# Dense attention beside sliding-window attention on one core: PV in groups of four column tiles, and dense matmuls placed by a count of active rows

## The chip, the core and the metric

The kernel runs on one core of a Trainium2 chip. A core has five engines that run side by side, each in its own program order: TensorE (PE, matrix products), VectorE (DVE), ScalarE (ACT), GpSimd (POOL) and SyncE (SP, which here only issues DMAs). They wait for one another through semaphores. PE writes into PSUM, eight banks of 128 partitions by 512 fp32 numbers; the other operands lie in SBUF.

The metric is the device time of one execution in microseconds, lower is better.

## The reference

Two attentions over 2048 positions and 448 features, with 16 heads of 28 features each; their outputs stand side by side in one result of 2048 x 896.

```python
def _A_ref(x, wq, wk, wv, wo):          # one key head and one value head for all 16 query heads
    q = (x @ wq).reshape(B, S, H, Dh).transpose(0, 2, 1, 3)
    k = x @ wk
    v = x @ wv
    p = softmax(einsum("bhqd,bkd->bhqk", q, k) * Dh ** -0.5)
    o = einsum("bhqk,bkd->bhqd", p, v)
    return o.transpose(0, 2, 1, 3).reshape(B, S, H * Dh) @ wo

def _B_ref(x, wqkv, wo):                # each position sees itself and 7 earlier ones, 2 apart
    q, k, v = heads of (x @ wqkv)
    kg, vg = k and v gathered at pos - 2 * w, w = 0..7
    attn = softmax(where(mask, einsum("bhsd,bhswd->bhsw", q, kg) * Dh ** -0.5, -1e9))
    return heads joined of einsum("bhsw,bhswd->bhsd", attn, vg) @ wo
```

Part A has 16 x 2048 x 2048 scores, all of which go through an exponential. Part B has eight scores a position and head.

## The kernel before, in words

**A planner writes each engine's program.** `Gen` lists every instruction (or small group of them) as an `Op` with an engine, an assumed duration, what it reads and writes, a priority `pr` and an earliest time `rel`. `Sched.run` then plays the program on a model of the five engines: whichever engine is free first takes the ready op with the lowest `pr`. The order found there is the order in which the engine executes, whatever the real durations turn out to be. `Sched.resolve` adds the semaphore waits.

**PSUM.** Part A's scores go into banks 0 to 2 and 3 to 4 in turn (`SLOTS`), its PV sums into bank 5 (`PVBANK`). Everything else shares banks 6 and 7 (`XBANKS`): a `Use` is one tenancy of such a bank, from its first PE op to its last reader.

**Part A** (`a_loop`, L655). There are 1024 units (sc, t, tb, j): 4 chunks of 512 queries, 4 groups t of four heads, 16 blocks of 128 keys, 4 heads j in a group. A unit is one scores matmul of 32 rows (a head's features) by 512 columns, and one PV matmul of 128 rows, 512 columns and 32 result columns. The units are cut into groups of three and of two, after the two slots. For each group n:

- the scores (L677): two or three matmuls, each in its own quarter of PE's rows, written to the slot's banks;
- the exponential (L688) on ACT, over 1536 or 1024 columns, out of PSUM into one of eight buffers (`expT`, `ERING`);
- PV (L702): the group's matmuls, each in its own quarter of PE's columns, added into bank 5. Where a group straddles two quads (a quad is the 64 units of one sc and t), PV is cut in two ops.

At the end of a quad `a_quad_end` copies bank 5 out (L722), sums the denominators (L727, Use "D"), inverts and spreads them (L733, L735), and scales (L741, L746); after every fourth quad come the output products (L758). Queries for the next chunk are projected by `a_q` (L629, L643).

**Part B** runs beside it in 16 blocks of 128 positions: projections of queries and keys for four blocks at a time (`b_qk`, L799) and of values (`b_v`, L815), products of queries and shifted keys on DVE (L840), their sums over a head by PE (`b_logits`, L847, 32 tiny matmuls a block), softmax, weighted values on DVE (L891), their sums by PE (L900), the output product (L907). Block k gets its earliest times from `T = B0 + BSTEP * k`.

**The start.** Ten matmuls on a tile of zeros (L535), A's first 512 positions transposed by PE, keys (`a_head`, L559), the value projection (`a_v`, L598), the keys' bias term (Use "KG", L604).

**Fills.** PE's granted clock depends on its recent work, so ahead of a scores group the planner may put one matmul whose result nobody reads (L675): if the dense ops that it booked in the last 2.2 us sum to under 0.3 us.

Of the kernel before, what the change touches and what calls it, by code (L numbers as in the profile page):

```python
# [12 lines left out]
D = 448  # L13
H = 16
DH = 28
KC = 112
NCH = 4
NSB = 16
WIN = 8
# [5 lines left out]
NU = 4 * 4 * 16 * 4  # L25
SLOTS = ((0, 1, 2), (3, 4))
EW = 512 * max(len(x) for x in SLOTS)
ERING = 8
# [29 lines left out]
class Use:  # L58


    def __init__(self, name, banks, late=False):
        self.name = name
        self.banks = banks
        self.late = late
        self.bank = None
        self.ops = []
        self.left = 0
        self.pe_left = 0


class Sched:
    LAT = 0.13
    OWN = 0.06
# [30 lines left out]
    def run(self, engines):  # L104
# [13 lines left out]
        recent = []  # L118

# [24 lines left out]
        while left:  # L144
# [3 lines left out]
            for (r, o) in cand[e]:  # L148
                bank = None
                if o.use is not None and o.use.bank is None:  # L150
                    ur = 0.0 if o.use.late else use_ready(o.use)
                    if ur is None:
                        continue
                    r = max(r, ur)
                    ok = [b for b in o.use.banks
                          if self.bank_busy[b] is None and (o.use.late or b not in self.claimed)]
                    if not ok:
                        continue
                    bank = min(ok, key=lambda b: self.bank_free_t[b])
                    r = max(r, self.bank_free_t[bank])  # L160
                if o.claims is not None:
                    if any(self.bank_busy[b] is not None for b in o.claims):
                        continue
                    r = max([r] + [self.bank_free_t[b] for b in o.claims])
                if r <= T + 1e-9:
                    key = (o.pr, o.idx)
                    if best is None or key < best[0]:
                        best = (key, o, bank)
                elif nxt is None or r < nxt:
                    nxt = r  # L170
            if best is None:
# [18 lines left out]
            if e == "pe":  # L190
                if o.fill is not None:
                    busy = sum(min(d, t1 - (T - 2.2)) for (t1, d) in recent if t1 > T - 2.2)
                    o.fill = busy < 0.3
                    if o.fill:
                        o.dur += 0.23
                        o.dense = 0.22
                if o.dense:
                    recent.append((T + o.dur, o.dense))
                    del recent[:-30]
# [103 lines left out]
class Gen:  # L303
# [227 lines left out]
    def a_head(self):  # L531
# [5 lines left out]
        for c in range(NCH):  # L537
            pr = -9 if c == 0 else c
            HB = g.HB if c == 0 else g.LB
            for h in range(2 if c == 0 else 0):  # L540
                u = Use(f"T{c}.{h}", HB)
                for kl in range(2):
                    for b in range(4):
# [4 lines left out]
                          R=["xst", "ident"], use=u, pr=pr, dense=0.055)  # L548
# [9 lines left out]
            for kt in range(4):  # L558
# [3 lines left out]
                  R=[("xT", c, kt), "wk4"], W=[u], use=u, pr=pr, rel=8.0 * min(c, 1), dense=0.21)  # L562
# [4 lines left out]
            else:  # L567
# [6 lines left out]
              R=[("k_sq", c % 2), "hq"], W=[u], use=u, pr=pr, dense=0.21)  # L574
# [10 lines left out]
    def a_v(self):  # L585
# [16 lines left out]
        u2 = Use("KG", g.LB)  # L602
# [13 lines left out]
    def a_q(self, sc, first=False):  # L616
# [3 lines left out]
        for t in range(4):  # L620
# [7 lines left out]
            for kt in range(4):  # L628
# [3 lines left out]
                  R=[("xT", sc, kt), ("wq4", t)], W=[u], use=u, pr=pr, rel=rel, dense=0.21)  # L632
# [4 lines left out]
            else:  # L637
# [8 lines left out]
              R=[("q_sq", t % 2), "hq"], W=[u], use=u, pr=pr if first else -1, rel=rel, dense=0.21)  # L646
# [9 lines left out]
    def a_loop(self):  # L656
# [5 lines left out]
        n, pos = -1, 0  # L662
        while pos < NU:
# [9 lines left out]
            def qk(e, us=us, b0=b0, box=[]):  # L673
                if box[0].fill:
                    e.matmul(g.bank(b0), g.ident[:, :], g.kT[:, 0:512], start=True, stop=True)  # L675
# [8 lines left out]
            o.fill = n > 4  # L684
# [8 lines left out]
            groups = []  # L693
            for i, x in enumerate(us):
                if groups and groups[-1][0] == x[:2]:
                    groups[-1][1].append((i, x))
                else:
                    groups.append((x[:2], [(i, x)]))
            for gi, (q, lst) in enumerate(groups):
                def pv(e, lst=lst, n=n):  # L700
                    for i, (sc, t, tb, j) in lst:
                        r = e.matmul(g.bank(PVBANK, p0=32 * j, p1=32 * j + 32), g.v_aug[:, tb, :],  # L702
                                     g.expT[:, n % ERING, 512 * i:512 * i + 512], start=tb == 0, stop=tb == 15,
                                     tile_position=(0, 32 * j))
                    return r
                o = a("pe", 0.32 if len(lst) > 1 else 0.3, pv, R=[("expT", n % ERING), "v_aug"], W=["pv"], pr=-40)
# [3 lines left out]
                sc, t = q  # L710
                if lst[-1][1][2:] == (15, 3):
                    g.a_quad_end(sc, t)

    def a_quad_end(self, sc, t):
# [10 lines left out]
        u = Use(f"D{sc}.{t}", XBANKS, late=last)  # L725
# [13 lines left out]
        for s4 in range(4):  # L739
# [3 lines left out]
              R=[("rrep", t % 2), "ident"], W=[u], use=u, pr=pr, dense=0.055)  # L743
# [7 lines left out]
        for s4 in range(4):  # L751
# [5 lines left out]
            for tt in range(4):  # L757
                o = a("pe", t_mm(D), lambda e, u=u, s4=s4, tt=tt: e.matmul(  # L758
                    g.bank(u.bank, D), g.oTn[:, tt, 128 * s4:128 * s4 + 128], g.wo4[:, tt, :], start=tt == 0, stop=tt == 3),
                  R=[("oTn", tt, s4 // 2), "wo4"], W=[u], use=u, pr=pr + s4 + tt if not last else -30 + tt, dense=0.19)  # L760
# [14 lines left out]
    BSTEP = 24.5  # L775
# [13 lines left out]
    def b_qk(self, c):  # L789
        g, a = self, self.s.add  # L790
        T = g.B0 + g.BSTEP * 4 * c
        for t in range(4):
            for w in range(2):
# [4 lines left out]
                for kt in range(4):  # L798
# [4 lines left out]
                      R=[("xT_B", kt), "wqkv"], W=[u], use=u, pr=pr, rel=rel, dense=0.21)  # L803
# [4 lines left out]
    def b_v(self, k):  # L808
# [5 lines left out]
        for kt in range(4):  # L814
# [3 lines left out]
              R=[("xT_B", kt), ("wvB", kt)], W=[u], use=u, pr=pr, rel=rel, dense=0.19)  # L818
# [8 lines left out]
    def b_logits(self, k):  # L827
# [55 lines left out]
    def b_out(self, k):  # L883
# [14 lines left out]
        for t in range(4):  # L898
            for w in range(4):
                a("pe", 0.09, lambda e, u=u, t=t, w=w: e.matmul(  # L900
                    g.bank(u.bank, 128, 128 * t, p1=KC), g.padd[:, w, KC * t:KC * t + KC], g.ident[:, :],
                    start=w == 0, stop=w == 3), R=["padd", "ident"], W=[u], use=u, pr=pr, dense=0.05)
# [3 lines left out]
        for t in range(4):  # L906
            a("pe", t_mm(D), lambda e, u=u, t=t: e.matmul(  # L907
                g.bank(u.bank, D), g.oT[:, k % 2, 128 * t:128 * t + 128], g.wo_B[:, t, :], start=t == 0, stop=t == 3),
              R=[("oT", k % 2), "wo_B"], W=[u], use=u, pr=pr, dense=0.19)
# [49 lines left out]
```

## Time and profile before

| | us |
|---|---|
| median of 3 runs | 537.56 |
| lowest, highest | 532.1, 560.13 |
| the profiled execution's own time | 533.57 |
| its span, first to last instruction | 531.7 |
| mean granted TensorE clock in the span | 0.922 |
| PE, ACT, DVE busy | 517.4, 481.0, 240.8 |

Times of single instructions come from the profiled execution. The profile gives for each engine when an instruction started and how long it took; matmul ends are modelled and overlap the next one's start, so the cost of a matmul is read from its start to the next one's start. "L677" is line 677 of the kernel. In a group's row, "x1024 | 168.3, 406" means 1024 instructions that cover 168.3 us, 406 ns each on average, and what follows the second bar is the engine's idle time just before them with what ended it. "PEclk" is the granted clock in tenths. A wait "PEld ps L677 <- ACT expT L688" is time in which PE's next weight load stood behind a semaphore that an exponential released.

### The profile page before, as it was taken

Reading aid. Unit: us, or ns where it says so; the run is one execution under the profiler, and the core shown is the slowest. Engines: PE = TensorE matmul, PEld = TensorE weight load, DVE = VectorE, ACT = ScalarE, POOL = GpSimd, SP = SyncE. Lnnn points to the kernel's source line nnn. Section 1 sums busy time; section 2 is a strip of 40 time slices with the busy share of each in tenths; the row PEclk is TensorE's granted clock in tenths of the full one; section 3 lists DMA queues with packets and bytes.
Section 4 is the critical chain, followed back from the end, with each engine's and each line's share of the span. In section 5 each row is a group of like instructions: output and inputs, shape, how many; then the busy total and the mean of one; then the engine's idle time right before and its main releaser. Section 6 shows DMA issues by size and latency. Waiting matters only on the chain.

```text
span 531.7 us, 8310 instructions
## 1 busy us (share of the span) xinstructions
PE 517.4 (97%) x3627; PEld 190.9 (36%) x3627; DVE 240.8 (45%) x400; ACT 481.0 (90%) x428; POOL 28.9 (5%) x43
## 2 busy tenths in 40 slices
PE   7999999999999999999999999999999999899997
PEld 2422343433434333333433333333344333333213
DVE  4524346653283458353842474366346542621002
ACT  3679999999999999999999999999999999866881
POOL 7020000100000010000100010010001000100000
PEclk9879999999999999999999999999999999755555
DMA  7870202001202032002002320110022212000001
GB/s 155 155 189 0 80 10 69 10 28 61 79 9 87 20 95 88 10 1 79 0 23 83 105 79 19 32 48 10 8 79 79 88 36 88 0 10 9 0 1 35
DMA packets 41587, 27.31 MB, mean 51 GB/s; under 512 B 17058, under 2 KB 41040, under 8 KB 41552
## 3 DMA queue, kind: packets, MB, share of 16 engines
q1 hardware_dynamic: 39600, 25.65, 16.9%
q10 hardware_dynamic: 1776, 0.81, 0.6%
q8 instruction: 28, 0.46, 0.4%
q0 software_dynamic: 176, 0.33, 0.3%
q14 instruction: 7, 0.06, 0.0%
HBM read 17.60 MB, written 5.52 MB: 43 GB/s over the span
## 4 chain that ended last, share of the span: by engine, by line
PE 62%; ACT 30%; DVE 3%; SPq 3%; issue 1%; DMA 1%; POOL 1%
ACT expT L688 29%; PE ps L677 17%; PE ps L702 17%; PE ps L799 8%; PE ps L675 4%; PE ps L629 3%; SPq L495 3%; PE ps L900 2%; PE ps L758 2%; PE ps L907 2%; PE ps L815 2%; PE ps L727 2%; PE ps L847 1%; DVE prod L891 1%; PE ps L741 1%
## 5 line engine op out<-in xcount | busy, mean ns | idle before, releaser
L688 ACT ACTIVATE expT<-ps 128x1536 bf16<-128x1536 f32 (+1 forms) x410 | 473.3, 1256 | 32.6 <-PE ps L677 24.6
L702 PE MATMUL ps<-expT,v_aug 128*32 128x512 bf16 x1024 | 169.3, 414 | 0.5 <-DVE PV_sb L722 0.5
L677 PE MATMUL ps<-qT,kT 32*128 32x512 bf16 x1024 | 168.3, 406 | 0.9 <-ACT expT L688 0.4
L702 PEld LDWEIGHTS ps<-expT,v_aug 128*32 128x32 bf16 x1024 | 39.8, 94 | 100.4 <-issue 96.9
L677 PEld LDWEIGHTS ps<-qT,kT 32*128 32x128 bf16 x1024 | 39.4, 91 | 92.2 <-issue 56.2
L840 DVE TENSOR_TENSOR stage<-qTB,kTB 112x1024 bf16<-112x1024 bf16 x64 | 44.3, 707 | 17.9 <-PE ps L847 17.7
L799 PE MATMUL ps<-xT_B,wqkv 128*112 128x512 bf16 (+1 forms) x128 | 46.6, 412 | 0.0
L675 PE MATMUL ps<-kT,ident 128*128 128x512 bf16 x91 | 39.5, 434 | 2.4 <-ACT expT L688 2.1
L735 POOL COPY rrep<-rden 128x512 bf16<-128x512 bf16 x15 | 14.7, 982 | 436.8 <-DVE rden L733 436.8
L891 DVE TENSOR_TENSOR prod<-Vsh,a_n 128x1792 bf16<-128x1792 bf16 x32 | 36.1, 1150 | 0.2
L900 PE MATMUL ps<-ident,padd 128*112 128x128 bf16 x256 | 28.9, 241 | 0.0
L847 PE MATMUL ps<-ones,stage 112*128 112x4 bf16 x512 | 27.3, 168 | 0.7 <-DVE Vst L819 0.7
L903 DVE CAST oT<-ps 112x512 bf16<-112x512 f32 x16 | 11.0, 689 | 36.6 <-PE ps L900 36.6
L847 PEld LDWEIGHTS ps<-ones,stage 112*128 112x128 bf16 x512 | 19.5, 96 | 19.9 <-issue 18.3
L900 PEld LDWEIGHTS ps<-ident,padd 128*112 128x112 bf16 x256 | 20.1, 138 | 15.1 <-issue 14.8
L733 DVE RECIPROCAL rden<-ps 128x16 bf16<-128x16 f32 x16 | 4.3, 272 | 42.7 <-PE ps L727 42.6
L799 PEld LDWEIGHTS ps<-xT_B,wqkv 128*112 128x112 bf16 (+1 forms) x128 | 14.5, 126 | 23.0 <-issue 21.5
L727 PEld LDWEIGHTS ps<-sel,PV_sb 128*128 128x128 f32 x128 | 19.4, 207 | 8.1 <-issue 7.4
L727 PE MATMUL ps<-sel,PV_sb 128*128 128x4 f32 x128 | 21.9, 267 | 0.1
L910 DVE CAST outB<-ps 128x448 bf16<-128x448 f32 x16 | 10.0, 624 | 26.2 <-PE ps L907 26.2
L629 PE MATMUL ps<-xT_A,wq 128*128 128x512 bf16 x64 | 21.5, 399 | 0.3 <-DVE wq L519 0.3
L758 PE MATMUL ps<-wo,oTn 128*128 128x448 bf16 x64 | 19.9, 411 | 0.5 <-DVE oTn L746 0.5
(99 smaller groups left out, 291.3 us busy)
## 6 DMA issues: line engine op xcount, KB each, us to landing
Vsh<-v_scratch SPq DMA_DIRECT2D x16, 896.0 KB, 4.6
v_scratch<-Vst SPq DMA_DIRECT2D x16, 112.0 KB, 1.7
out_dram<-outB SPq DMA_DIRECT2D x16, 112.0 KB, 1.7
out_dram<-outA SPq DMA_DIRECT2D x14, 112.0 KB, 1.7
wqkv<-in_B_wqkv_dram SPq DMA_DIRECT2D x1, 1008.0 KB, 5.7
stage<-in_A_x_dram ACTq DMA_DIRECT2D x1, 448.0 KB, 3.5
wo_B<-in_B_wo_dram SPq DMA_DIRECT2D x4, 98.0 KB
wo<-in_A_wo_dram SPq DMA_DIRECT2D x4, 98.0 KB
```

What stands on the lines that cost most here:

```text
L629: a("pe", t_mm(512), lambda e, u=u, t=t, kt=kt: e.matmul(g.bank(u.bank), g.wq4[64 * (kt // 3):, t, kt, :], g.xT_A[64 * (kt // 3):, kt, 512 ...
L675: e.matmul(g.bank(b0), g.ident[:, :], g.kT[:, 0:512], start=True, stop=True)
L677: r = e.matmul(g.bank(b0 + i), g.kT[32 * j:32 * j + 32, 128 * tb:128 * tb + 128], g.qT[32 * j:32 * j + 32, sc % 2, t, :], start=True, stop ...
L688: x = a("act", t_exp(w), lambda e, b0=b0, w=w, n=n: e.activation(g.expT[:, n % ERING, 0:w], g.ps[:, 512 * b0:512 * b0 + w], ACT.Exp, scale ...
L702: r = e.matmul(g.bank(PVBANK, p0=32 * j, p1=32 * j + 32), g.v_aug[:, tb, :], g.expT[:, n % ERING, 512 * i:512 * i + 512], start=tb == 0, s ...
L727: a("pe", 0.25, lambda e, u=u, s4=s4: e.matmul(g.bank(u.bank, 4, 4 * s4), g.PV_sb[:, t, 128 * s4:128 * s4 + 128], g.sel4[:, :], start=True ...
L758: o = a("pe", t_mm(D), lambda e, u=u, s4=s4, tt=tt: e.matmul(g.bank(u.bank, D), g.oTn[:, tt, 128 * s4:128 * s4 + 128], g.wo4[:, tt, :], st ...
L799: a("pe", t_mm(512), lambda e, u=u, t=t, kt=kt, w=w: e.matmul(g.bank(u.bank, p1=KC), g.wqkv[64 * (kt // 3):, kt, w * D + KC * t:w * D + KC ...
L840: op = a("dve", t_dve_2x(1024), lambda e, t=t, qv=qv, kv=kv: e.tensor_tensor(out=g.prodT[0:KC, t, :, :], in0=qv, in1=kv, op=ALU.mult), R=R ...
L847: a("pe", 0.06, lambda e, u=u, t=t, w=w: e.matmul(g.bank(u.bank, 128).rearrange("p (h w) -> p h w", w=WIN)[:, 4 * t:4 * t + 4, w], g.prodT ...
L891: a("dve", t_dve_2x(4 * D), lambda e, hf=hf, Vv=Vv, av=av: e.tensor_tensor(out=g.prod2[:, 4 * hf:4 * hf + 4, :].rearrange("p w (d h) -> p ...
L900: a("pe", 0.09, lambda e, u=u, t=t, w=w: e.matmul(g.bank(u.bank, 128, 128 * t, p1=KC), g.padd[:, w, KC * t:KC * t + KC], g.ident[:, :], st ...
```

## The change

1. **PV in fours.** `a_loop` collects the units over group borders and issues PV for four at a time, one in each quarter of PE's columns. A quad has 16 such groups and none is cut.
2. **A new measure.** `dense` is no longer a duration but a number of columns: 512 or 448 for a full matmul, 128 for a scores group, 700 for a PV group, 128 for small square ones. `area` is the sum booked in the last `WIN` = 2.2 us, per us; `WANT` is 1200.
3. **Fills by that measure.** Ahead of a scores group come none, one or two fills (now on the tile of zeros). Where PE would idle in the plan for over 0.12 us and the measure is under `WANT`, a fill goes into a free one of banks 5 to 7. Ahead of the ops of Uses "KG", "D" and "L", which use 128 columns of their bank, a fill of 384 columns may go into the bank's other columns.
4. **Logits in blocks of four** matmuls an op (L847) instead of single ones, and `BSTEP` from 24.5 to 26.

```diff
 class Sched:
     LAT = 0.13
+    WIN = 2.2
+    WANT = 1200.0
+    FILL = None
...
+        def area(T):
+            return sum(d for (t1, d) in recent if t1 > T - self.WIN) / self.WIN
...
+            if best is None and e == "pe" and self.FILL and T > 4 and (nxt is None or nxt > T + 0.12) and area(T) < self.WANT:
+                ok = [b for b in (PVBANK,) + XBANKS if self.bank_busy[b] is None and b not in self.claimed and self.bank_free_t[b] <= T]
+                if ok and left > 40:
+                    o = Op("pe", 0.23, None, 0, 0, "fill")
+                    o.emit = self.FILL(ok[0])
+                    o.dense = 512
...
             if e == "pe":
-                if o.fill is not None:
-                    busy = sum(min(d, t1 - (T - 2.2)) for (t1, d) in recent if t1 > T - 2.2)
-                    o.fill = busy < 0.3
-                    if o.fill:
-                        o.dur += 0.23
-                        o.dense = 0.22
+                if o.use is not None and o.use.spare and area(T) < self.WANT:
+                    o.fill = 1
+                    o.dur += 0.18
+                    o.dense += 512 - o.use.spare
+                elif o.fill is not None:
+                    o.fill = max(0, min(2, round((self.WANT - area(T)) * self.WIN / 512 + 0.3)))
+                    o.dur += 0.22 * o.fill
+                    o.dense += 512 * o.fill
...
+            self.s.FILL = lambda b: (lambda e: e.matmul(
+                self.bank(b), self.warm[:, 0:128], self.warm[:, :], start=True, stop=True))
...
+                        if o.fill and o.use is not None:
+                            lo = o.use.spare
+                            eng.matmul(self.bank(o.use.bank, 512 - lo, lo), self.warm[:, 0:128], self.warm[:, lo:512],
+                                       start=True, stop=True)
...
-        u2 = Use("KG", g.LB)
+        u2 = Use("KG", g.LB, spare=128)
...
             def qk(e, us=us, b0=b0, box=[]):
-                if box[0].fill:
-                    e.matmul(g.bank(b0), g.ident[:, :], g.kT[:, 0:512], start=True, stop=True)
+                for _ in range(box[0].fill):
+                    e.matmul(g.bank(b0), g.warm[:, 0:128], g.warm[:, :], start=True, stop=True)
...
-            o.fill = n > 4
+            o.fill = 0
+            o.dense = 128
...
-            groups = []
             for i, x in enumerate(us):
-                if groups and groups[-1][0] == x[:2]:
-                    groups[-1][1].append((i, x))
-                else:
-                    groups.append((x[:2], [(i, x)]))
-            for gi, (q, lst) in enumerate(groups):
-                def pv(e, lst=lst, n=n):
-                    for i, (sc, t, tb, j) in lst:
-                        r = e.matmul(g.bank(PVBANK, p0=32 * j, p1=32 * j + 32), g.v_aug[:, tb, :],
-                                     g.expT[:, n % ERING, 512 * i:512 * i + 512], start=tb == 0, stop=tb == 15,
+                where.append((x, n % ERING, i))
+            while len(where) >= 4 or (where and pos == NU):
+                grp, where = where[:4], where[4:]
+                sc, t, tb, _ = grp[0][0]
+
+                def pv(e, grp=grp):
+                    for (sc, t, tb, j), r, i in grp:
+                        x = e.matmul(g.bank(PVBANK, p0=32 * j, p1=32 * j + 32), g.v_aug[:, tb, :],
+                                     g.expT[:, r, 512 * i:512 * i + 512], start=tb == 0, stop=tb == 15,
                                      tile_position=(0, 32 * j))
...
-                o = a("pe", 0.32 if len(lst) > 1 else 0.3, pv, R=[("expT", n % ERING), "v_aug"], W=["pv"], pr=-40)
+                o = a("pe", 0.33, pv, R=[("expT", r) for r in sorted({y[1] for y in grp})] + ["v_aug"], W=["pv"], pr=-40,
+                      dense=700)
...
-        u = Use(f"D{sc}.{t}", XBANKS, late=last)
+        u = Use(f"D{sc}.{t}", XBANKS, late=last, spare=128)
...
-    BSTEP = 24.5
+    BSTEP = 26.0
...
-        u = Use(f"L{k}", XBANKS)
+        u = Use(f"L{k}", XBANKS, spare=128)
         for t in range(4):
-            for w in range(WIN):
-                a("pe", 0.06, lambda e, u=u, t=t, w=w: e.matmul(
-                    g.bank(u.bank, 128).rearrange("p (h w) -> p h w", w=WIN)[:, 4 * t:4 * t + 4, w],
-                    g.prodT[0:KC, t, w, :], g.ones4[:, :], start=True, stop=True),
-                  R=[("prodT", t), "ones4"], W=[u], use=u, pr=pr)
+            for w0 in (0, 4):
+                def lgs(e, u=u, t=t, w0=w0):
+                    for w in range(w0, w0 + 4):
+                        r = e.matmul(g.bank(u.bank, 128).rearrange("p (h w) -> p h w", w=WIN)[:, 4 * t:4 * t + 4, w],
+                                     g.prodT[0:KC, t, w, :], g.ones4[:, :], start=True, stop=True)
+                    return r
+                a("pe", 0.2, lgs, R=[("prodT", t), "ones4"], W=[u], use=u, pr=pr)
```

The remaining lines give the other matmuls their `dense` in columns (512, 448, 256, 128 or 112) in place of a duration.

More of the change, by code (lines that the diff above doesn't have):

```diff
@@ L58, with __init__ @@
 class Use:
-    def __init__(self, name, banks, late=False):
+    def __init__(self, name, banks, late=False, spare=None):
         self.name = name
@@ L170, in run @@
                     nxt = r
+            if best is None and e == "pe" and self.FILL and T > 4 and (nxt is None or nxt > T + 0.12) and area(T) < self.WANT:
[4 more added lines that the diff above has]
+                    o.dense = 512
+                    o.idx = len(self.ops)
+                    o.nd = 0
+                    o.deps = set(self.bank_last[ok[0]])
+                    self.bank_last[ok[0]] = {o}
+                    self.bank_free_t[ok[0]] = T + 0.23
+                    self.ops.append(o)
+                    left += 1
+                    best = (None, o, None)
             if best is None:
@@ L547, in a_head @@
                             g.xst[:, b, x0:x0 + 128], g.ident[:, :]),
-                          R=["xst", "ident"], use=u, pr=pr, dense=0.055)
+                          R=["xst", "ident"], use=u, pr=pr, dense=128)
                 dst = g.xT_A[:, 2 * h:2 * h + 2, 0:512]
@@ L645, in a_q @@
                 skip_group_check=True),
-              R=[("q_sq", t % 2), "hq"], W=[u], use=u, pr=pr if first else -1, rel=rel, dense=0.21)
+              R=[("q_sq", t % 2), "hq"], W=[u], use=u, pr=pr if first else -1, rel=rel, dense=512)
             if first and t == 0:
@@ L661, in a_loop @@
         g.last_exp = {}
-        n, pos = -1, 0
+        n, pos, where = -1, 0, []
         while pos < NU:
@@ L742, in a_quad_end @@
                 g.bank(u.bank, 128, 128 * s4), lhs, g.ident[:, :], start=True, stop=True),
-              R=[("rrep", t % 2), "ident"], W=[u], use=u, pr=pr, dense=0.055)
+              R=[("rrep", t % 2), "ident"], W=[u], use=u, pr=pr, dense=128)
         for hf in range(2 if last else 1):
@@ L802, in b_qk @@
                         tile_position=(64 * (kt // 3), 0)),
-                      R=[("xT_B", kt), "wqkv"], W=[u], use=u, pr=pr, rel=rel, dense=0.21)
+                      R=[("xT_B", kt), "wqkv"], W=[u], use=u, pr=pr, rel=rel, dense=512)
                 dst = g.kTB[:, t, PAD + 512 * c:PAD + 512 * c + 512] if w else g.qTB[:, c % 2, t, :]
@@ L817, in b_v @@
                 start=kt == 0, stop=kt == 3, tile_position=(64 * (kt // 3), 0)),
-              R=[("xT_B", kt), ("wvB", kt)], W=[u], use=u, pr=pr, rel=rel, dense=0.19)
+              R=[("xT_B", kt), ("wvB", kt)], W=[u], use=u, pr=pr, rel=rel, dense=448)
         a("dve", t_dve_ps(D), lambda e, u=u: e.tensor_copy(out=g.Vst[:, k % 2, :], in_=g.bank(u.bank, D)),
@@ L901, in b_out @@
                     g.bank(u.bank, 128, 128 * t, p1=KC), g.padd[:, w, KC * t:KC * t + KC], g.ident[:, :],
-                    start=w == 0, stop=w == 3), R=["padd", "ident"], W=[u], use=u, pr=pr, dense=0.05)
+                    start=w == 0, stop=w == 3), R=["padd", "ident"], W=[u], use=u, pr=pr, dense=112)
         a("dve", t_dve_ps(512), lambda e, u=u: e.tensor_copy(out=g.oT[:, k % 2, :], in_=g.bank(u.bank, p1=KC)),
```

18 lines of the change are left out of this document (9 added, 9 removed).

## The prediction

> **What bounds the kernel now.** I began with the page: busy time, slices, groups.
>
> ```profile
> span 531.7 us, 8310 instructions
> PE 517.4 (97%) x3627; PEld 190.9 (36%) x3627; DVE 240.8 (45%) x400; ACT 481.0 (90%) x428; POOL 28.9 (5%) x43
> ...
> PEclk9879999999999999999999999999999999755555
> ...
> L688 ACT ACTIVATE expT<-ps 128x1536 bf16<-128x1536 f32 (+1 forms) x410 | 473.3, 1256 | 32.6 <-PE ps L677 24.6
> ...
> L675 PE MATMUL ps<-kT,ident 128*128 128x512 bf16 x91 | 39.5, 434 | 2.4 <-ACT expT L688 2.1
> ```
>
> Two engines look full. ACT's work is nearly all the exponentials (L688): 473.3 us that the change doesn't touch, with 32.6 us of idle time ahead of them. That idle time is the prize. PE's 97% is an average of stages with different clocks, so next I asked for the busy time by stage, cut at the first exponential (12.4), where the granted clock falls (458.8) and at the last exponential's end (519.4). After each stretch and its length stand the busy times of PE, weight loads, DVE, ACT and POOL, then the granted clock.
>
> ```profile
> 0.00:12.40 12.40, 9.96 (x47) 3.65 (x47) 5.67 (x19) 4.40 (x7) 10.35 (x24) 1.00 0.79 157
> 12.40:40.00 27.60, 25.59 (x190) 9.90 (x189) 11.52 (x23) 19.94 (x18) 3.79 (x4) 0.81 0.80 170
> 40.00:458.80 418.80, 412.42 (x3107) 156.79 (x3105) 212.68 (x343) 409.00 (x364) 14.11 (x14) 1.00 0.15 48
> 458.80:519.40 60.60, 60.60 (x261) 16.48 (x259) 8.25 (x12) 45.93 (x38) 0.62 (x1) 0.50 0.01 4
> 519.40:531.70 12.30, 8.80 (x32) 4.10 (x30) 2.69 (x6) 1.71 (x4) 0.00 (x0) 0.50 0.12 37
> ```
>
> ACT's idle time is 27.60 - 19.94 = 7.7 us in the start, 418.80 - 409.00 = 9.8 in the middle and 60.60 - 45.93 = 14.7 in the last stage. The middle is ACT's: it works 97.7% of it. The last stage is PE's: granted clock 0.50, PE busy without a gap, ACT waiting for scores. So nearly half of the prize is a clock that fell because little dense work was left.
>
> What does the planner's new measure say of that fall? I count by the weights of the diff: 128 for a scores op, 700 for four PV tiles (175 each), a dense matmul's columns. Two adjoining stretches of 3.41 us, the second ending at the fall:
>
> ```profile
> L702 PE MATMUL ps<-expT,v_aug 128*32 128x512 bf16 x8 | 1.2, 389 | 0.0
> L677 PE MATMUL ps<-qT,kT 32*128 32x512 bf16 x8 | 1.2, 384 | 0.0
> L675 PE MATMUL ps<-kT,ident 128*128 128x512 bf16 x2 | 0.8, 382 | 0.0
> ...
> L702 PE MATMUL ps<-expT,v_aug 128*32 128x512 bf16 x8 | 1.4, 451 | 0.0
> L677 PE MATMUL ps<-qT,kT 32*128 32x512 bf16 x5 | 0.8, 384 | 0.0
> L675 PE MATMUL ps<-kT,ident 128*128 128x512 bf16 x1 | 0.4, 390 | 0.2 <-ACT expT L688 0.2
> L741 PE MATMUL ps<-ident,rrep 128*128 128x128 bf16 x2 | 0.3, 224 | 1.3 <-POOL rrep L735 1.3
> ```
>
> First: 8 x 175 + 3 x 128 + 2 x 512 = 2808 in 3.41 us, 823 per us. Second: 1400 + 256 + 512 + 256 = 2424, 711 per us, and the clock falls. The plan asks for 1200. ACT runs slower than planned, which dilutes that: 15 exponentials, about 7.5 pairs, take 17.49 us, so 2.33 us a pair, where the planner's formula gives 2.23. That leaves some 1150, still well above 823.
>
> ```profile
> 198.94 17.49 ACT L688 ACTIVATE expT<-ps 128x1536 bf16<-128x1536 f32 x15 [0.79 <-PE ps L677]
> ```
>
> The new fills read a tile of zeros. Zeros count: the clock was already 1.00 in the first row of the stages, after nothing but this:
>
> ```profile
> 1.26 3.60 PE L535 MATMUL ps<-warm 128*128 128x512 bf16 x8 [1.26 <-DVE warm L440]
> ```
>
> **The change, part by part.**
>
> **PV in fours.** There are 410 score groups, and so 410 PV ops plus 9 that a quad's end cuts in two (64 units a quad, slots of 3 and 2: the cut lies inside a slot at 9 of 15 ends): 419. Afterwards 1024 / 4 = 256. What a four costs is already in the trace, at one quad's end:
>
> ```profile
> 205.96 0.40 PE L702 MATMUL ps<-expT,v_aug 128*32 128x512 bf16 x4
> 206.29 0.39 PE L677 MATMUL ps<-qT,kT 32*128 32x512 bf16 x2
> ```
>
> Start to next start: 0.33 us for four tiles; the next rows give the same for three (61.20 to 61.53) and for two (62.20 to 62.53). So 163 ops x 0.32, the smaller rounding, are 52 us of PE time that go. A four waits for up to two exponentials and holds a buffer up to one slot longer; the ring has eight, so after the start I cost this at nothing. Without that cover the next exponential would wait for a buffer.
>
> On the path these 52 us are worth only what ACT waits for. Where dense projections stand between scores, it does wait:
>
> ```profile
> 60.88 0.39 PE L677 MATMUL ps<-qT,kT 32*128 32x512 bf16 x3
> 61.20 0.40 PE L702 MATMUL ps<-expT,v_aug 128*32 128x512 bf16 x3
> 61.53 0.42 PE L799 MATMUL ps<-xT_B,wqkv 128*112 128x512 bf16 x1
> ...
> 62.20 0.39 PE L702 MATMUL ps<-expT,v_aug 128*32 128x512 bf16 x2
> 62.53 1.13 PE L799 MATMUL ps<-xT_B,wqkv 128*112 128x512 bf16 x3
> 63.59 0.39 PE L677 MATMUL ps<-qT,kT 32*128 32x512 bf16 x3
> ```
>
> A pair takes 63.59 - 60.88 = 2.71 us here against ACT's 2.33: 0.38 lost. PV's share falls from 2 x 0.32 to 1.25 x 0.33, by 0.23, three fifths of the loss.
>
> **Fills.** What does one cost, and how many come?
>
> ```profile
> 443.14 0.54 PE L815 MATMUL ps<-wvB,xT_B 128*128 128x448 bf16 x2
> 443.62 0.39 PE L677 MATMUL ps<-qT,kT 32*128 32x512 bf16 x3
> ...
> 445.57 0.39 PE L675 MATMUL ps<-kT,ident 128*128 128x512 bf16 x1
> 445.90 0.39 PE L677 MATMUL ps<-qT,kT 32*128 32x512 bf16 x3
> ```
>
> A fill alone between tiled ops takes 0.33 us; two dense matmuls in a row 0.48, 0.24 each. The plan books 0.22 or 0.23 a fill. The Trainium skill (TensorEngine Tiling (Array Packing), Key Properties) says that changing the tiling mode drains the engine, which speaks against scattering fills singly; 0.33 beside 0.24 agrees with it.
>
> Their number is an estimate from the diff: 1200 over some 500 us is 600,000 columns. Scores give 410 x 128 = 52,000, PV 256 x 700 = 179,000, B 16 x 9,470 = 152,000, A's projections 16 x 4,860 = 78,000: together 461,000. The missing 139,000 are 271 fills of 512. Rich stretches lend nothing to poor ones, so up to 400. At 0.24 to 0.33 us that is 65 to 132 us of PE time. The room: 52 from PV, 30 from the 91 old fills (x 0.33), and what PE waits for ACT in the middle:
>
> ```profile
> PEld ps L677 <- ACT expT L688: 26.4, 88, 0.5
> ...
> PEld ps L675 <- ACT expT L688: 5.9, 20, 0.5
> ```
>
> 26.4 + 5.9 = 32, so some 114 us of room. It mostly fits. Middle: I take 4 of its 9.8 us as won (the projections' share), bounds all 9.8 won and 10 more lost (the upper count at the dear price overruns the room by 18 us, about half of it where ACT waits).
>
> **The last stage.** With the clock held, a pair needs 2 x 0.32 for scores, 1.25 x 0.33 for PV and three fills (0.33 + 2 x 0.33 at most): 2.04 us against ACT's 2.33. So ACT binds; I take 12.7 of the 14.7 us, bounds 0 and all. The step from 24.5 to 26 per B block delays B's last block by 15 x 1.5 = 22 us, which covers the stage's start with real work, and B still ends ahead of A. Its output DMAs move along on SP's queue, with nothing due behind them.
>
> **After the last exponential** 12.3 us pass at clock 0.50.
>
> ```profile
> 522.50 1.71 PE L727 MATMUL ps<-sel,PV_sb 128*128 128x4 f32 x8
> ```
>
> PE is busy for 8.80 of them; the sums (this row), the last products and the matmuls queued ahead of them are about 5 us on the path, an estimate. Half would go at full clock: 2.5. Bounds 0 and 8.80 / 2 = 4.4.
>
> **The start.** ACT's one long gap, 5.5 us, ends when the first PV frees the ring, late at half clock:
>
> ```profile
> 26.76 2.00 PE L629 MATMUL ps<-xT_A,wq 128*128 128x512 bf16 x4
> 28.68 1.89 PE L702 MATMUL ps<-expT,v_aug 128*32 128x512 bf16 x15
> 29.34 2.37 ACT L688 ACTIVATE expT<-ps 128x1536 bf16<-128x1536 f32 x2 [5.50 <-PE ps L702]
> ```
>
> Fills in idle time should keep the clock, worth 2 to 3 us here. But up to two fills before each score op, and one before each of the 16 KG ops while the measure is low, stand in the same queue ahead of V, whose matmuls the measure doesn't count: 8 to 10 fills, 2 to 3 us. Net nothing, bounds 4 won and 3 lost. Blocks of four logits instead of single ones: nothing, PE's order alone hides it; bounds 1 us each way.
>
> **The sum**, against the profiled execution's 533.57: 0 - 4 - 12.7 - 2.5 = -19.2, so 514.4; I say 514. The runs shown have a median of 537.56, 4 us above that execution. A difference of 2%, about 10.7 us, is what a measurement of this kernel can tell from no change.
>
> **Rivals.**
>
> *Fills bind PE.* Clock held (-12.7 - 2.5), but the middle loses its 10 us: 528. For it: the plan books 0.23 for what costs 0.33. Against: 32 us of waiting, and ACT 4% slower than planned.
>
> *The clock falls all the same.* The Trainium skill (TensorE: Matmul & The Clock Gate, Part 1, What's actually happening) ties the clock to how busy PE has been in a window of about 3.4 us. Read as busy time, the rule speaks against fills: this trace has PE busy 60.60 of 60.60 us at 0.50, so by it a fuller PE gains nothing. Worked out from rows: with fills at half clock each op takes 0.54,
>
> ```profile
> 482.17 0.61 PE L675 MATMUL ps<-kT,ident 128*128 128x512 bf16 x1
> 482.71 0.61 PE L677 MATMUL ps<-qT,kT 32*128 32x512 bf16 x3
> ```
>
> so a pair takes (2 + 1.25 + 3) x 0.54 = 3.4 us, 31% of it lost to ACT. B's later end leaves 39 us of it: 12 lost in place of 14.7, so 533.6 - 4 - 2.7 = 527.
>
> *It falls earlier and stays down: the slower end.* The place is a light stretch between two B rounds; after a fall the fills themselves are the load, and the same 31% runs to the end. Saved elsewhere are 4 + 14.7, so it turns slower from 19 / 0.31 = 60 us at half clock, by over 2% from 95. With 130 us it is 533.6 - 18.7 + 40 = 555. Against it: the clock did come back once, at 32.2, after 3.41 us whose 19 PV tiles alone are 3325, 975 per us.
>
> ```profile
> L702 PE MATMUL ps<-expT,v_aug 128*32 128x512 bf16 x19 | 2.4, 598 | 0.0
> ```
>
> **How the numbers follow.** Forecast (504 to 521): 0.65. Fills bind PE (528): 0.16. Clock falls all the same (527): 0.11. Falls early (545 and more): 0.08. The floor with every bound won is 533.6 - 4 - 9.8 - 14.7 - 4.4 = 501. Range 503 to 531: it takes in the first three cases but for their ends. Faster by over 2%: the forecast and, since the two middle rivals lie near the line, 0.10 of their 0.27: 0.75. Within 2%: 0.17. Slower: 0.08.
>
> **What would show it.** PEclk 9 or more in every slice up to the last; PV's row x1024 with fours throughout the timeline; 270 to 400 fills in place of 91; ACT's idle time before L688 near 15 us; the last stage's ACT at 9 tenths or more. Wrong if the slices show a 5, or if ACT idles more than now in the middle (9.8 us).

## The result and the profile after

The changed kernel takes 515.3 us (median of 4 runs, 509.35 to 519.08) beside 536.47 for the kernel before, a ratio of the medians of 0.961. The ratios given with a 95% interval, here 0.9555 (0.9412 to 0.9697), compare the faster executions of each kernel alone. The profiled execution took 517.55 us. In the page of the changed kernel the last slices of the granted clock have no 5 any more; the lowest are a 6 in the start and a 6 in the middle, where the clock dips:

```profile
span 515.1 us, 8657 instructions
PE 478.2 (93%) x3773; PEld 186.4 (36%) x3827; DVE 239.2 (46%) x400; ACT 478.5 (93%) x428; POOL 25.8 (5%) x43
...
PEclk9769999999999999999699999999999999999999
...
L718 ACT ACTIVATE expT<-ps 128x1536 bf16<-128x1536 f32 (+1 forms) x410 | 470.8, 1261 | 18.2 <-PE ps L706 11.9
...
L731 PE MATMUL ps<-expT,v_aug 128*32 128x512 bf16 x1024 | 102.9, 397 | 0.1
```

PV is now line 731, the scores 706, the exponentials 718. PV covers 102.9 us in place of 169.3. The same cut into stages, with the dip a stage of its own (columns as before):

```profile
12.33:40.00 27.67, 26.27 (x182) 10.45 (x185) 12.44 (x25) 17.26 (x16) 3.80 (x4) 0.75 0.76 169
40.00:245.60 205.60, 196.01 (x1577) 76.86 (x1596) 108.51 (x178) 200.40 (x178) 5.45 (x7) 1.00 0.14 47
245.60:255.90 10.30, 9.62 (x51) 3.72 (x52) 5.40 (x7) 6.55 (x6) 0.26 (x1) 0.50 0.01 2
255.90:458.80 202.90, 188.96 (x1578) 74.47 (x1599) 91.65 (x150) 200.44 (x179) 5.38 (x7) 1.00 0.16 51
458.80:506.77 47.97, 42.29 (x318) 14.55 (x320) 12.90 (x19) 47.85 (x44) 0.62 (x1) 1.00 0.02 6
506.77:515.10 8.33, 4.11 (x28) 1.93 (x26) 2.59 (x6) 1.57 (x3) 0.00 (x0) 1.00 0.17 55
```

ACT's idle time, before and after: in the start 7.7 and 10.4 us; from 40 to 458.8 us 9.8 and 11.4 (5.2 + 3.75 + 2.5, the middle one in the 10 us of the dip); in the last stage 14.7 and 0.1. What follows the last exponential fell from 12.3 to 8.3 us. Together that is +2.7 + 1.6 - 14.6 - 4.0 = -14.3 of the 16.6 us between the spans. The rest lies in ACT's busy time, 2.5 us less for the same instructions: one exponential takes as long as before (1261 ns in place of 1256), but they cover 470.8 us in place of 473.3, since those that follow one another closely overlap more.

The waits show what PE's freed time became: PE stands before a fill or a scores group until ACT is done (48.9 + 26.4 us), where before it was 28.4 and 9.7.

```profile
PEld ps L706 <- ACT expT L718: 48.9, 137, 0.9
...
PEld ps L704 <- ACT expT L718: 26.4, 63, 0.9
```

The spread between executions goes with the clock. The kernel before ranged from 511.92 us at a mean clock of 0.989 to 584.61 at 0.815 beside the last set of experiments; the changed kernel stayed between 509.35 (1.000) and 519.08 (0.977) in ten runs. Two of the 35 runs of the kernel before lie in that range too: 511.92, and 517.31 at a clock of 0.973. Where its clock held, it was as fast; at 0.987 and 0.985 the changed kernel took 513.4. So what the change buys is that the clock holds through nearly all of every execution. At a held clock these runs show no gain.

### The profile page after: what moved, and what is told of

It is laid out like the page before. It is cut to its first block, busy times and chain, and to the rows that moved or that the text cites. A ratio compares the mean times of both kernels' runs of the same rounds, so it can differ in the third digit from the quotient of the medians.

```text
span 515.1 us, 8657 instructions
## 1 busy us (share of the span) xinstructions
PE 478.2 (93%) x3773; PEld 186.4 (36%) x3827; DVE 239.2 (46%) x400; ACT 478.5 (93%) x428; POOL 25.8 (5%) x43
## 4 chain that ended last, share of the span: by engine, by line
ACT 55%; PE 37%; SPq 3%; DVE 2%; issue 2%; DMA 1%; POOL 0%
ACT expT L718 55%; PE ps L706 10%; PE ps L828 7%; PE ps L731 6%; PE ps L704 3%; SPq L524 3%; PE ps L931 2%; PE ps L658 2%; PE ps L844 2%; PE ps L756 1%; PE ps L361 1%; PE ps L938 1%; DVE prod L922 1%; PE ps L627 1%; PE ps L878 1%
## 5 line engine op out<-in xcount | busy, mean ns | idle before, releaser
L718 ACT ACTIVATE expT<-ps 128x1536 bf16<-128x1536 f32 (+1 forms) x410 | 470.8, 1261 | 18.2 <-PE ps L706 11.9
L706 PE MATMUL ps<-qT,kT 32*128 32x512 bf16 x1024 | 161.3, 389 | 14.0 <-ACT expT L718 9.2
L731 PE MATMUL ps<-expT,v_aug 128*32 128x512 bf16 x1024 | 102.9, 397 | 0.1
L704 PE MATMUL ps<-warm 128*128 128x512 bf16 x114 | 41.8, 393 | 11.2 <-ACT expT L718 9.4
L731 PEld LDWEIGHTS ps<-expT,v_aug 128*32 128x32 bf16 x1024 | 26.2, 93 | 59.1 <-issue 57.1
L764 POOL COPY rrep<-rden 128x512 bf16<-128x512 bf16 x15 | 11.7, 781 | 435.1 <-DVE rden L762 435.1
L890 DVE TENSOR_REDUCE mx<-ps 128x16 f32<-128x128 f32 x15 | 4.4, 291 | 50.4 <-PE ps L878 50.4
L931 PE MATMUL ps<-ident,padd 128*112 128x128 bf16 x256 | 25.9, 233 | 0.6 <-DVE padd L925 0.6
L338 PE MATMUL ps<-warm 128*128 128x512 bf16 x75 | 24.4, 384 | 1.4 <-issue 0.6
L704 PEld LDWEIGHTS ps<-warm 128*128 128x128 bf16 x143 | 12.5, 104 | 28.7 <-ACT expT L718 26.4
L658 PE MATMUL ps<-xT_A,wq 128*128 128x512 bf16 (+1 forms) x57 | 19.7, 396 | 1.5 <-issue 1.5
L848 DVE CAST Vst<-ps 128x448 bf16<-128x448 f32 x16 | 10.0, 622 | 23.4 <-PE ps L844 23.4
```

The source lines that it names most:

```text
L338: self.s.FILL = lambda b: (lambda e: e.matmul(self.bank(b), self.warm[:, 0:128], self.warm[:, :], start=True, stop=True))
L658: a("pe", t_mm(512), lambda e, u=u, t=t, kt=kt: e.matmul(g.bank(u.bank), g.wq4[64 * (kt // 3):, t, kt, :], g.xT_A[64 * (kt // 3):, kt, 512 ...
L704: e.matmul(g.bank(b0), g.warm[:, 0:128], g.warm[:, :], start=True, stop=True)
L706: r = e.matmul(g.bank(b0 + i), g.kT[32 * j:32 * j + 32, 128 * tb:128 * tb + 128], g.qT[32 * j:32 * j + 32, sc % 2, t, :], start=True, stop ...
L718: x = a("act", t_exp(w), lambda e, b0=b0, w=w, n=n: e.activation(g.expT[:, n % ERING, 0:w], g.ps[:, 512 * b0:512 * b0 + w], ACT.Exp, scale ...
L731: x = e.matmul(g.bank(PVBANK, p0=32 * j, p1=32 * j + 32), g.v_aug[:, tb, :], g.expT[:, r, 512 * i:512 * i + 512], start=tb == 0, stop=tb = ...
```

## The experiments

**Each half alone.** First PV in fours and nothing else, in the kernel before:

```diff
-            for gi, (q, lst) in enumerate(groups):          # one PV op for each score group
+            while len(where) >= 4 or (where and pos == NU): # one PV op for four units
```

> The kernel before with PV in fours and nothing else (old rule for the fills, old pace of B, single logits). Theory 1, the gain is the held clock: the clock still falls near the place where B ends and stays at 0.50 for some 50 to 60 us, ACT idles 6 to 15 us in that stage, 522 to 530 us in all. Theory 2, the gain is PE time freed by PV: at half clock a pair needs 2 x 0.54 + 1.25 x 0.54 + one old fill of 0.54 = 2.3 us, ACT's own 2.33, so the last stage loses under 3 us although its clock is 0.50, and the whole is 512 to 518 us, as with all of the change.

Measured: 666.12 us (627.08 to 694.27), against 537.58 for the kernel before. Neither theory saw that. The page of this kernel:

```profile
span 666.8 us, 8371 instructions
PE 644.9 (97%) x3656; PEld 205.3 (31%) x3656; DVE 240.7 (36%) x400; ACT 498.4 (75%) x428; POOL 26.4 (4%) x43
...
PEclk9675555555559955898556755765855585555557
...
L688 ACT ACTIVATE expT<-ps 128x1536 bf16<-128x1536 f32 (+1 forms) x410 | 490.1, 1237 | 152.1 <-PE ps L677 143.2
```

The clock is at 5 tenths from the start on, not only in the last stage, and ACT waits 143.2 us for scores. Fewer PV ops free PE's time, and by that they seem to take away the work that held the clock, although the plan put in 120 of the old fills here in place of 91. Now the other half, the changed kernel with PV as before:

```diff
-                o = a("pe", 0.33, pv, R=[("expT", r) for r in ...] + ["v_aug"], W=["pv"], pr=-40, dense=700)
+                o = a("pe", 0.32 if len(lst) > 1 else 0.3, pv, R=[...], W=["pv"], pr=-40, dense=175 * len(lst))
```

> The changed kernel with PV as before (two or three tiles an op, 419 ops in place of 256; the measure books 175 a tile). It has 259 fills. Theory, PV in fours pays for the fills: PE needs 163 x 0.32 = 52 us more, where the changed kernel's waits for ACT leave about 75 us; with fills at the wrong places ACT waits in the middle, 15 to 30 us more idle than the changed kernel, 525 to 545 us, clock 0.98 or more. Rival, the fills alone bring the gain: 511 to 520 us.

Measured: 531.02 us (528.34 to 533.95 in 10 runs), mean clock 0.983 in the profiled one. The kernel before took 535.81 in the same set. The clock is held, and the time is PE's, though not in ACT's waits in the middle, where the theory had it: ACT is idle for only 10.5 us from 40 to 458.8.

```profile
40.00:458.80 418.80, 416.52 (x3063) 156.05 (x3062) 188.42 (x305) 408.35 (x360) 10.31 (x12) 1.00 0.13 42
```

And its timeline (start, length, engine, instruction) near the end:

```profile
509.84 0.60 ACT L749 ACTIVATE PV_sb<-ps 128x512 f32<-128x512 f32 x1 [0.74 <-PE ps L732]
...
526.83 0.93 PE L939 MATMUL ps<-wo_B,oT 112*128 112x448 bf16 x4 [0.79 <-DVE oT L935]
```

PE is busy 416.52 of 418.80 us; A's last PV sum is read at 509.84, but B's last products are still running at 526.83. B, which has the lower priority, pays. So PV in fours buys the time in which the fills run, and the fills buy the clock that PV in fours would cost. Each half needs the other. (The logits in blocks of four, which this kernel keeps, had no run of their own.)

**No fills, and fills on a quarter of the rows.** The changed kernel with `WANT = 0`:

> The changed kernel with its measure set to want nothing: no fill anywhere. Theory 1, the fills hold the clock: it falls in the last stage and several times in the middle, wherever PE has mostly sums, logits and scores; 525 to 545 us. Theory 2, PV in fours frees PE enough that a half clock matters little: a pair without fills needs 3.25 x 0.54 = 1.8 us even at 0.50, below ACT's 2.33; then only stretches with dense work lose, and it is 510 to 520 us, not slower than the changed kernel.

Measured: 636.57 us (626.71 to 644.84), ratio 1.18 (1.157 to 1.203) to before.

```profile
PEclk9575555698556557995557555555555855555557
```

The slices show half clock over most of the span. A stretch of the timeline, PE alone:

```profile
300.08 0.61 PE L706 MATMUL ps<-qT,kT 32*128 32x512 bf16 x3
300.62 0.99 PE L931 MATMUL ps<-ident,padd 128*112 128x128 bf16 x7
301.54 0.61 PE L706 MATMUL ps<-qT,kT 32*128 32x512 bf16 x2
302.08 0.62 PE L731 MATMUL ps<-expT,v_aug 128*32 128x512 bf16 x4
302.63 0.36 PE L931 MATMUL ps<-ident,padd 128*112 128x128 bf16 x1
302.92 0.61 PE L706 MATMUL ps<-qT,kT 32*128 32x512 bf16 x3
```

A pair takes 302.92 - 300.08 = 2.84 us here, against ACT's 2.33: at half clock B's own work no longer fits between the scores. My second theory had allowed for stretches with dense work alone; these seven matmuls are B's small sums. Theory 1 has the sign and the place; its size, 10 to 30 us over the changed kernel, is far short of the 121 measured.

Is it enough that PE is busy? The same fills at the same places, on 32 of 128 rows:

```diff
-                    e.matmul(g.bank(b0), g.warm[:, 0:128], g.warm[:, :], start=True, stop=True)
+                    e.matmul(g.bank(b0), g.warm[32 * j0:32 * j0 + 32, 0:128], g.warm[32 * j0:32 * j0 + 32, :],
+                             start=True, stop=True, tile_position=(32 * j0, 0))
```

(and likewise for the other two kinds, on the first quarter of the rows; j0 is the quarter of the group's first score)

> The changed kernel with the same fills at the same places, but each uses 32 of PE's rows in place of 128 (same columns, about the same time, or less where it runs beside a scores tile). If the clock follows active rows: the fills weigh a quarter, the last stage counts about 256 + 875 + 3 x 128 = 1500 in 2.33 us, 650 per us, below the 711 at which it fell before, so the clock falls to 0.50 in the last stage and in the middle, and ACT loses there: 520 to 545 us. If it follows how long PE is busy: as the changed kernel, 509 to 519 us, clock 0.97 or more.

Measured: 715.92 us (680.11 to 731.76), the slowest of all.

```profile
PE 701.1 (98%) x3827; PEld 220.3 (31%) x3827; DVE 241.2 (34%) x400; ACT 502.0 (70%) x428; POOL 25.9 (4%) x43
...
PEclk9797557555555555555555757655565755555556
```

Its groups by line:

```profile
L704 PE MATMUL ps<-warm 32*128 32x512 bf16 x143 | 74.0, 571 | 1.8 <-ACT expT L719 1.4
```

The fills are there (L704, x143 as in the changed kernel's weight loads). PE is busy 98% of the span and the clock is at half for most of it (0.58 on average). So the clock doesn't follow busy time; the rows that a matmul uses count, as the change's words say. Fills on few rows only cost.

**How much to want.** `WANT` at 800 (138 fills), 1600 (465 fills), 1200 being 291:

> The changed kernel with 800 wanted in place of 1200 (138 fills in place of 291). Theory, the clock falls where a window of 3.4 us counts under some 900 per us: 800 lies below, the clock falls many times in the middle, 530 to 580 us. Rival, 1200 has margin to spare: fewer fills, clock held, 507 to 514 us.

> The changed kernel with 1600 wanted (465 fills in place of 291). Theory, PE's room ends there: 174 fills more at 0.24 to 0.33 us are 42 to 57 us of PE time against waits for ACT of about 75 us, and fills ahead of scores stand in the chain; clock 1.00 from 40 us on, but ACT idles 10 to 25 us more in the middle, 520 to 540 us. Rival, there is room: no dips any more, 507 to 512 us.

Measured: 604.44 us (580.14 to 622.47) at 800, and 528.35 (525.08 to 533.47) at 1600. The slices of the granted clock at 800, then at 1600:

```profile
PEclk9799995999999999855586579975669555555557
```

```profile
PEclk9759999999999999999999999999999999999999
```

At 800 the clock falls in many places, and more is lost than the theory had; that much lower there is no margin. At 1600 it holds from the start's end on, and the fills cost 13 us. In the middle ACT's idle time is 15.3 us, and the start is longer too, 14.0 us of ACT's idle time in place of 10.4, 7.0 of them in one wait. So the rival, that there is room, is refuted. Stages and waits at 1600:

```profile
12.33:40.00 27.67, 27.16 (x175) 10.42 (x171) 10.15 (x20) 13.69 (x13) 3.67 (x4) 0.69 0.80 169
40.00:458.80 418.80, 415.07 (x3305) 158.18 (x3304) 203.32 (x329) 403.50 (x355) 11.04 (x14) 1.00 0.14 45
```

```profile
ACT gcol L636 <- PE ps L633: 7.0, 1, 7.0
```

**B's pace**, `BSTEP = 24.5` in the changed kernel:

> The changed kernel with B's old pace (24.5 in place of 26 a block, so B ends some 22 us earlier; 290 fills). Theory, the fills hold the clock and not B's later end: the last stage stays at clock 1.00 and ACT at 9 tenths or more, the whole within 4 us of the changed kernel, 509 to 519. Rival, the pace matters: the clock falls after B's end and ACT loses 8 to 15 us there, 522 to 530.

Measured: 510.98 us (509.40 to 515.85), ratio 0.9579 (0.9512 to 0.9646). In the last stage the clock is at 1.00 and ACT works 41.68 of 42.00 us:

```profile
458.80:500.80 42.00, 36.60 (x246) 10.97 (x246) 1.64 (x3) 41.68 (x38) 0.62 (x1) 1.00 0.00 1
```

DVE's 1.64 us show that B is over there, so there the fills hold the clock and not B's later end. Beside the fills the new pace is worth nothing.

**The start.** The fills there stand ahead of the keys' bias and the value projection. Without them:

```diff
-            ... self.FILL and T > 4 and ...
+            ... self.FILL and T > 30 and ...          # and T > 30 for the other two kinds
```

> The changed kernel without any fill before 30 us of the plan (none in idle time, ahead of scores or in the spare columns). Theory: the changed kernel's start is 2.7 us longer than before because some ten fills stand ahead of the value projection and the keys' bias at half clock; without them ACT's idle time up to 40 us falls from 10.4 us to 7 or 8, and the whole by 2 to 4 us, to about 510 to 514. Rival: the clock falls in the start in either case and the late value projection sets the first PV, so the fills there cost nothing: same start within 1 us.

Measured: 512.82 us (512.34 to 514.90), ratio 0.9613 (0.953 to 0.9696). ACT works 19.33 of the start's 27.67 us, 2.1 more than in the changed kernel's profiled execution. But a second profile of the changed kernel, from the last set below, has 19.41 with all its fills. So the rival holds: the fills in the start cost nothing that these runs show, and the 2.1 us belong to one execution, whose clock came back at 34.0 us, against 31.6 in the second profile and 31.5 without the fills. The stage without the fills, then that of the second profile; and PE's timeline without them:

```profile
12.33:40.00 27.67, 25.82 (x183) 9.69 (x182) 14.32 (x26) 19.33 (x18) 3.85 (x4) 0.72 0.78 169
12.33:40.00 27.67, 26.75 (x198) 10.61 (x197) 13.83 (x26) 19.41 (x18) 3.87 (x4) 0.88 0.77 169
```

```profile
26.53 2.00 PE L658 MATMUL ps<-xT_A,wq 128*128 128x512 bf16 x4
28.45 2.33 PE L731 MATMUL ps<-expT,v_aug 128*32 128x512 bf16 x20
```

The clock falls there all the same (0.72), and four query projections at half clock still stand ahead of the first PV. The last set ran the changed kernel once more, then that start with these projections later (`rel` 17 to 24), then B's old pace on top, then 1100 wanted on top of that.

> The changed kernel once more, beside the next three on the same chip: 509 to 519 us, its spread due to dips of the clock in the middle that come in some executions and not in others.

> The changed kernel with no fill before 30 us of the plan, and the first chunk's query projections t = 1 to 3 not before 24 us of the plan instead of 17, so that they no longer stand ahead of the first PV (2.0 us at half clock there). Theory, PE's queue ahead of the first PV sets the start: ACT's idle time up to 40 us falls from 8.3 us (no fills, old place) to 6 or 7, and the whole to 509 to 512. Rival, the value projection's end and the DVE step behind it set it: no gain over 512.8.

> The same start, and B's old pace of 24.5 as well: both single gains add up to 506 to 510 us. Rival: the two overlap, 509 to 512.

> The same with 1100 wanted in place of 1200 (229 fills). If 1200 has some margin: 505 to 509 us at the same clock. If it sits at the edge, as the dips of the changed kernel speak for: several dips of 10 us at half clock in most executions, 3 to 4 us lost in each, 512 to 530 us.

Measured, in the same order: 512.31 us (509.45 to 517.31), 524.42 (512.65 to 553.74), 512.18 (507.72 to 535.06), 519.04 (509.55 to 535.52). The gap ahead of the first PV did shrink, from 4.1 us without the fills to 2.98, as the theory has it. But ACT's idle time up to 40 us did not fall to 6 or 7 in the profiled executions of the second and third kernel (9.4 and 9.1 us), only in the fourth's (5.7). Neither the second's total nor the third's came down as forecast, and some executions lost far more, since the clock came back late, in the profiled one of the second kernel at 129 us. Its slices, and ACT's timeline at the gap:

```profile
PEclk9555555558999999999999997799999999999998
```

```profile
28.24 4.62 ACT L718 ACTIVATE expT<-ps 128x1536 bf16<-128x1536 f32 x4 [2.98 <-PE ps L731]
```

In three profiled executions with this same start the clock came back at 129.0, 45.8 and 29.5 us. With the fills left out and the projections in their old place it came back at 31.5, and those four runs stayed within 512.34 to 514.90. So a late return was seen only with the moved projections on top of the missing fills, and not each time; no run moved the projections alone. At 1100 wanted the profiled execution had two dips after the start, of 48 and 7 us (its clock was 0.936), as the second case of its expectation has it. None of the variants beats the changed kernel beyond the spread: its 512.3 stands beside 511.0 with B's old pace and 512.2 for the third, which has the lowest single run (507.72) and one of 535.06.

## Why the prediction was right, and where it wasn't

The forecast was 514 with a range of 503 to 531; the profiled execution came to 517.55, the median to 515.3. The mechanism that carried the sum, **the clock held in the last stage**, was right and a little better than booked: 14.6 us won where 12.7 stood, ACT working 47.85 of 47.97. **After the last exponential** 4.0 us went where 2.5 stood; the eight sum matmuls took 1.05 us in place of 1.71 and had fewer matmuls queued ahead of them.

**The start** was mis-sized: booked at nothing, it lost 2.7 us in this execution, near the end of its bound (3 lost); in the second profile it lost 0.6. The step "fills in idle time should keep the clock" failed: the clock fell at about 20 us (0.75 over the stage, 0.81 before), and the fills ahead of KG then ran at half clock. The waits of ACT in the start, of which the first, 4.3 us, was not there before:

```profile
ACT gcol L636 <- PE ps L633: 4.3, 1, 4.3
ACT expT L718 <- PE ps L731: 4.2, 1, 4.2
```

**The middle** was mis-sized too: 4 us won on paper, 1.6 lost in this execution, 3.75 of it in the dip. In an execution without a dip, the changed kernel's second profile, ACT works 410.91 of 418.80 us, so the middle won 1.9:

```profile
40.00:458.80 418.80, 403.31 (x3282) 155.27 (x3280) 208.26 (x339) 410.91 (x365) 11.09 (x14) 1.00 0.15 48
```

The number of fills was as estimated, 291 against 271 to 400, and outside the dip ACT, not PE, bound the middle. That a four waits for up to two exponentials was misread: cut from groups of three and two, 51 of the 256 wait for three. It cost nothing, as booked: after the start ACT waits for scores alone. The rival that fills bind PE (528) came true only where PV's savings were taken away or 465 fills put in.

Of the signs named ahead, the slices show no 5, but a 7 and two 6 where every one was to be 9, and ACT idled 11.4 us in the middle, over the 9.8 that were to mean wrong. In the second profile, without a dip, it is 7.9 in the middle, and 13.9 ahead of all exponentials, near the 15 that were named.

The step that failed in kind lies under all of this: **the weights**. I counted a PV tile as 175 wherever it stood, so that three groups before the change (8 tiles) weighed 1400, and read from it a fall between 711 and 823 per us with a wide margin under 1200. By that count PV in fours changes the load not at all. The runs say otherwise: fours alone cost 129 us, at a clock of 0.613. The dip in the changed kernel speaks against the reading too. This is the stretch of 3.41 us that ends where the clock falls (245.6); four of its eight PV tiles start before it, and the five scores are two ops:

```profile
L828 PE MATMUL ps<-xT_B,wqkv 128*112 128x512 bf16 (+1 forms) x4 | 1.4, 411 | 0.0
L756 PE MATMUL ps<-sel,PV_sb 128*128 128x4 f32 x6 | 0.8, 256 | 0.0
L731 PE MATMUL ps<-expT,v_aug 128*32 128x512 bf16 x8 | 0.8, 390 | 0.0
L706 PE MATMUL ps<-qT,kT 32*128 32x512 bf16 x5 | 0.8, 384 | 0.0
```

By the prediction's weights, with nothing for the six sums of 4 columns, that is 2048 + 700 + 256 = 3004, 880 per us, or 805 if the one projection matmul on 64 rows counts half. So the clock fell about where it had held before (823), and what was to leave "some 1150" left 880 at most.

A count over all stretches of 3.41 us at full clock in the 14 traces points the same way (some 1,580, some 60 of them followed by a fall; the times between the clock's changes are whole multiples of this length). The best single threshold misjudges about 30 with 175 a tile, and about 20 with 600 a PV op however many tiles it has and 64 a scores op plus 64 a scores tile; that threshold lies at 800 to 850. This is a fit to the same traces with weights chosen for it, not an experiment, and the dip above, 907 by it or 832 with the 64 rows at half, lies at its edge. By it the two stretches in the prediction are 1800 + 704 + 1024 = 3528, 1034 per us, and 1200 + 448 + 512 + 256 = 2416, 708. (Five of the second's eight PV tiles start in it, in two ops; with these the prediction's own weights give 557 and not 711.) So the margin was thinner than I said, and a PV op in two or three tiles may itself have been a fill. That 1200 was enough was in part luck: 1100 beside the changed start gave dips and 519.04, 800 gave 604.44. On this reading the forecast was right because the plan's own count, 700 a four, is near what a four weighs, while my reading of the kernel before had got its PV groups too light.

**Rivals.** The one that the clock falls all the same is refuted by the quarter-row fills as far as it rests on busy time: PE 98% busy, clock 0.58 on average, 716 us. The Trainium skill (TensorE: Matmul & The Clock Gate, Part 1, What's actually happening) ties the clock to how busy PE has been; read as busy time, these runs do not agree with it. The two states that this section names agree with every trace here: stretches are at 1.00 or 0.50 only. The slow rival, a fall that keeps itself up, had the right mechanism. It didn't come in the changed kernel, whose one dip of 10 us ended by itself. But the kernel without fills in the start and with its projections later stayed down for 113 us; from 30 to 129 us, with the fills in place, PE was busy 98.97 of 99.00 us at 0.50. The last rule, a drain between tiling modes (the Trainium skill, TensorEngine Tiling (Array Packing), Key Properties), agrees with the changed kernel's timeline: a fill between tiled ops takes 0.33 us. That a drain is the cause is not shown.

```profile
483.49 0.39 PE L704 MATMUL ps<-warm 128*128 128x512 bf16 x1 [0.19 <-ACT expT L718]
483.82 0.39 PE L706 MATMUL ps<-qT,kT 32*128 32x512 bf16 x3
```

## What to carry to other kernels

Before packing small matmuls more tightly, look at what holds the clock: an op saved can be load lost, and on this kernel the packing alone cost 24%, while the packing with fills gained 4% by holding the clock. Read the granted clock beside the busy time, stage by stage, and test a suspected load by a variant that keeps the time and drops the rows. Where executions of one kernel differ by several per cent, put their clocks beside their times first.

## What was not expected of the hardware

With the fills on 32 rows PE is 98% busy and its clock is at half for most of the span (0.58 on average). By the fit above, a PV op on all 128 rows seems to weigh about the same with two, three or four column tiles side by side. And a fall can last: 160 us and more at 0.50 in the kernel with PV in fours alone, while PE was busy for 158.82 of them. The stage:

```profile
40.00:200.00 160.00, 158.82 (x774) 46.43 (x773) 57.26 (x92) 106.77 (x90) 2.91 (x3) 0.50 0.09 28
```
